# Decode attention kernel: closing barrier removed, output split into early and late DMAs (the last head by columns), identity matmul ahead of two V pieces

## The chip, the cores and the metric

The kernel runs on one core of one Trainium2 chip. The metric is the device time of one execution in microseconds (us). A profiled execution also has a span, from its first to its last record, which is 1 to 2 us shorter than the time. Engines are PE (matmul), PEld (its weight loads), DVE (vector), ACT (scalar), POOL (GpSimd) and SP, which here only issues DMAs; SPq is SP's queue of DMA issues.

## The reference

```python
B, Hq, Hkv, Sq, Sk, D = 1, 32, 8, 1, 65536, 128      # q, k, v in bfloat16
k = jnp.repeat(k, Hq // Hkv, axis=1); v = jnp.repeat(v, Hq // Hkv, axis=1)
scores = jnp.einsum("bhqd,bhkd->bhqk", q, k) * D ** -0.5
return jnp.einsum("bhqk,bhkd->bhqd", _softmax(scores), v)
```

K and V are 134 MB each and are read once. The output is 32 rows of 128 bfloat16, 8 KB.

## The kernel before

K and V of each of the 8 KV heads come in two blocks of 8 MB, so there are N = 16 blocks. A block is 256 "tiles" of 128 x 128. DVE transposes K, PE makes the scores, ACT takes them out of PSUM and exponentiates, PE multiplies by V. There are two K buffers but only one V buffer, so V is refilled behind PE. The last two V blocks (14 and 15) are loaded in halves: a half may be loaded as soon as PE has used that half of the block before. `pv_s` counts the halves that PE has used.

The parts that matter (cuts marked):

```python
KLAST = (64, 64, 64, 64)          # pieces of the last K block, in tiles
VLAST = (64, 32, 16, 8, 8)        # pieces of the second half of the last V block
NEND = 2                          # so many of them after the identity matmul
# ... SP, the load queue
        def load_v(i):
            if i < N - HALVED: ...            # whole block, once PE has used all of block i-1
            sp.wait_ge(pv_s, 2 * i - 1)       # first half of block i-1 used
            load(vbuf, vf, i, 0, TH, va_in)
            sp.wait_ge(pv_s, 2 * i)           # second half of block i-1 used
            ...
        load_k(0)
        for j in range(1, N + 1):
            if j < N:
                load_k(j)
            load_v(j - 1)
        sp.wait_ge(ox_s, 1)
        sp.dma_start(of.rearrange("h (a i) -> a h i", a=A), oX).then_inc(o_out, 16)
        sp.wait_ge(o_out, 16)
# ... PE, after its loop: adds the first block's rescaled sum to the accumulator
        pe.matmul(acc[:, 0:R], lhsT=ident, rhs=o2, start=False, stop=False)
        for n, a, b in list(pieces(VLAST, TH))[-NEND:]:
            pe.wait_ge(vlast_in[n], 16)
            values(range(a, b))
# ... DVE, last step of its loop over heads, then what follows the loop
                    dv.wait_ge(pv_s, h * (2 * C) + 2)             # ALL of block 14, for the last head
                    dv.tensor_copy(o1, acc[:, 0:R]).then_inc(co_s, 1)
        weigh(H - 1); divisor(H - 1)
        dv.wait_ge(pv_s, 2 * N)
        dv.tensor_tensor(oT[:, Hq - R:Hq], acc[:, 0:R], recip, ALU.mult).then_inc(fin_s, 1)
        dv.wait_ge(fin_s, H)
        dv.transpose(oX, oT).then_inc(ox_s, 1)
```

`oT` holds the output as columns, 128 partitions by 32 query rows. Blocks of 32 x 32 are transposed into `oX`, so that one DMA can write the output as 128 runs of 64 bytes. The engines' programs stand in a block with a barrier at its end.

Of the kernel before, what the change touches and what calls it, by code (L numbers as in the profile page):

```python
# [11 lines left out]
S4 = 32  # L12
T = 256
TG = 16
# [3 lines left out]
NK = 2  # L18
NKT = 2
FIRST = (64, 64, 128)  # L20
KLAST = (64, 64, 64, 64)
VLAST = (64, 32, 16, 8, 8)
NEND = 2
HALVED = 2


def bass_standalone__gqa_softmax__decode_kernel(nc, q, k, v, out):
    B, Hq, Sq, D = q.shape
    _, H, Sk, _ = k.shape
    R = Hq // H  # L30
    CK = P * T
# [4 lines left out]
    A = P // S4  # L36
    NB, NE = 2, 2
    W = T // U * R
    TH = T // 2
    QH = NB * NE * A * R  # L40
    scale = float(D) ** -0.5
    assert sum(VLAST) == TH and sum(VLAST[-NEND:]) == TG

    kf, vf = k[0], v[0]
    qf, of = q[0, :, 0, :], out[0, :, 0, :]

    es = ExitStack()
    S = es.enter_context
# [12 lines left out]
    oT, oX = oTX[:, 0:Hq], oTX[:, Hq:]  # L61
# [23 lines left out]
    def sem(name):  # L85
        return S(nc.semaphore(name))
# [3 lines left out]
    first_in = [sem(f"first_in{i}") for i in range(len(FIRST))]  # L90
    klast_in = [sem(f"klast_in{i}") for i in range(len(KLAST))]
    vlast_in = [sem(f"vlast_in{i}") for i in range(len(VLAST))]
    q_in, o_out = sem("q_in"), sem("o_out")
    tr_s, qk_s, mv_s, mx_s, hm_s = sem("tr_s"), sem("qk_s"), sem("mv_s"), sem("mx_s"), sem("hm_s")
    hma_s, nb_s, df_s, wg_s, ex_s, pv_s = sem("hma_s"), sem("nb_s"), sem("df_s"), sem("wg_s"), sem("ex_s"), sem("pv_s")
    ls_s, co_s, ow_s, rw_s, rh_s, rc_s, fin_s = (
        sem("ls_s"), sem("co_s"), sem("ow_s"), sem("rw_s"), sem("rh_s"), sem("rc_s"), sem("fin_s"))
    ox_s, tail_s = sem("ox_s"), sem("tail_s")
    init_s, pool_s, qt_s, qb_s, warm_s = sem("init_s"), sem("pool_s"), sem("qt_s"), sem("qb_s"), sem("warm_s")

    def src(t, i):
        h, c = divmod(i, C)
        return t[h, c * CK:(c + 1) * CK, :].rearrange("(p t) d -> p (t d)", p=P)

    def pieces(sizes, at=0):
        for n, size in enumerate(sizes):
            yield n, at, at + size
            at += size

    block = S(nc.Block())  # L110

    @block.sync
    def _(sp):
        def load(buf, t, i, a, b, s):
            sp.dma_start(buf[:, a * D:b * D], src(t, i)[:, a * D:b * D]).then_inc(s, 16)  # L115

        def load_k(i):
            if i >= NK:
                sp.wait_ge(tr_s, (i - NK + 1) * G)
            if i in (0, N - 1):  # L120
                for n, a, b in pieces(FIRST if i == 0 else KLAST):
                    load(kbuf[i % NK], kf, i, a, b, (first_in if i == 0 else klast_in)[n])
            else:
                load(kbuf[i % NK], kf, i, 0, T, k_in[i % NK])

        def load_v(i):
            if i < N - HALVED:
                if i >= 1:
                    sp.wait_ge(pv_s, 2 * i)
                load(vbuf, vf, i, 0, T, v_in)  # L130
                return
            sp.wait_ge(pv_s, 2 * i - 1)
            load(vbuf, vf, i, 0, TH, va_in)
            sp.wait_ge(pv_s, 2 * i)
            if i < N - 1:
                load(vbuf, vf, i, TH, T, vb_in)
            else:
                for n, a, b in pieces(VLAST, TH):
                    load(vbuf, vf, i, a, b, vlast_in[n])

        load_k(0)
        for j in range(1, N + 1):
            if j < N:
                load_k(j)
            load_v(j - 1)
        sp.wait_ge(ox_s, 1)
        sp.dma_start(of.rearrange("h (a i) -> a h i", a=A), oX).then_inc(o_out, 16)
        sp.wait_ge(o_out, 16)

    @block.gpsimd  # L150
    def _(g):
# [24 lines left out]
    @block.tensor  # L176
    def _(pe):
        def scores(g, qcols):


            kt = ktb[g % NKT][:, :].rearrange("p (b n e) -> p b e n", b=NB, e=NE)
            for n in range(TG // A):
                at = (g % GU * (TG // A) + n) * A * R
                for be in range(NB * NE):
                    ins = pe.matmul(  # L185
                        qkb[g // GU][:, at:at + A * R],
                        lhsT=kt[:, be // NE, be % NE, n * P:(n + 1) * P],
                        rhs=qblk[:, bass.ds(qcols[be], A * R)],
                        start=be == 0, stop=be == NB * NE - 1,
                    )  # L190
            ins.then_inc(qk_s, 1)

        def values(tiles):

            for t in tiles:
                ins = pe.matmul(  # L196
                    acc[:, 0:R], lhsT=vbuf[:, t * D:(t + 1) * D], rhs=pts[:, t * R:(t + 1) * R],
                    start=t == 0, stop=t == T - 1,
                )
                if t % TH == TH - 1:  # L200
                    ins.then_inc(pv_s, 1)


        turn, skip, skipl, late, last, kept, whole = (
            pe.alloc_register(name) for name in ("turn", "skip", "skipl", "late", "last", "kept", "whole"))
        pe.reg_mov(turn, 0)
        pe.wait_ge(qb_s, A * NB)
        with nc.Fori(
            0, N + 1, 1, engines=bass.OrderedEngineSet([pe.engine]), head_slot={pe.engine: 0},
        ) as it:  # L210
            pe.reg_alu(skip, it, 1, ALU.is_lt)
            pe.reg_alu(last, it, N, ALU.is_ge)
            pe.reg_alu(late, it, N - HALVED + 1, ALU.is_ge)
            pe.reg_add(skipl, skip, last)
            pe.reg_alu(kept, it, N - 1, ALU.min)
            pe.reg_alu(whole, it, N - HALVED, ALU.min)
            kept_ = pe.snap(kept, min_val=0, max_val=N - 1)
            whole_, late_, last_ = (pe.snap(r, min_val=0, max_val=N) for r in (whole, late, last))
            hq = kept_ // C * QH
            qcols = [hq + be * A * R for be in range(NB * NE)]  # L220
            with pe.If_lt(turn, N):
                for g in range(G):
                    if g % GU == 0:
                        pe.wait_ge(mv_s, it * U + (g // GU + 1))
                    pe.wait_ge(tr_s, it * G + (g + 1))
                    scores(g, qcols)
            with pe.If_eq(skip, 0):
                pe.wait_ge(co_s, it - 1)
                pe.wait_ge(ex_s, it * R)
                pe.wait_ge(v_in, whole_ * 16)  # L230
                pe.wait_ge(va_in, late_ * 16 + last_ * 16)
                values(range(TH))
                pe.wait_ge(vb_in, late_ * 16)
                for n, a, b in list(pieces(VLAST, TH))[:-NEND]:
                    pe.wait_ge(vlast_in[n], last_ * 16)
                    values(range(a, b))
            with pe.If_eq(skipl, 0):
                values(range(T - TG, T))
            pe.reg_add(turn, turn, 1)


        pe.wait_ge(tail_s, 2)
        pe.wait_ge(ow_s, H)
# [5 lines that stand above are left out]
    @block.vector  # L249
    def _(dv):  # L250
# [28 lines left out]
        def weigh(h):  # L279

            dv.wait_ge(wg_s, h + 1)
            dv.wait_ge(co_s, h * C + 1)
            dv.tensor_tensor(o2, o1, wgt, ALU.mult).then_inc(ow_s, 1)  # L283
            dv.wait_ge(ex_s, h * (R * C) + R * C)
            dv.tensor_tensor(rhead, rsum[0], wgt, ALU.mult).then_inc(rw_s, 1)  # L285
            dv.wait_ge(rw_s, h + 1)
            dv.tensor_tensor(rhead, rsum[1], rhead, ALU.add).then_inc(rh_s, 1)  # L287

        def divisor(h):
            dv.wait_ge(ls_s, h + 1)  # L290
            dv.reciprocal(recip, lsum).then_inc(rc_s, 1)  # L291
            dv.wait_ge(rc_s, h + 1)
# [4 lines left out]
        started, before, filled, last = (  # L297
            dv.alloc_register(name) for name in ("started", "before", "filled", "last"))


        with nc.Fori(0, H, 1, engines=bass.OrderedEngineSet([dv.engine]), head_slot={dv.engine: 0}) as h:  # L301
# [8 lines left out]
            for b in range(C):  # L310
                dv.wait_ge(k_in[b], (filled_ if b else h) * 16)
                moved = h * (C * U) + (U + b * U + 1)
                for g in range(G):
                    for n, at, _ in pieces(KLAST if b else FIRST):
                        if at == g * TG:
# [21 lines left out]
                else:  # L337
                    with dv.If_eq(started, 1):
# [5 lines left out]
                        dv.wait_ge(co_s, h * C)  # L344
                        dv.tensor_tensor(oT[:, bass.ds(before_ * R, R)], o2, recip, ALU.mult).then_inc(fin_s, 1)  # L345

        weigh(H - 1)
        divisor(H - 1)
        dv.wait_ge(pv_s, 2 * N)
        dv.tensor_tensor(oT[:, Hq - R:Hq], acc[:, 0:R], recip, ALU.mult).then_inc(fin_s, 1)  # L350
        dv.wait_ge(fin_s, H)
        dv.transpose(oX, oT).then_inc(ox_s, 1)

    @block.scalar
    def _(ac):
# [68 lines left out]
```

## Time and profile before

| | before |
|---|---|
| time, first three runs | 631.56 us median (630.2 to 631.56) |
| span | 628.3 us |
| moved | 268.60 MB, 427 GB/s over the span |
| busy PE, DVE, ACT | 43%, 54%, 44% |

The executions fall into two groups 1.3 us apart (630.2 and 631.5). Differences below 1 us are therefore hard to see.

The page's view in 40 equal slices has the busy share of the DMA engines in tenths, and the rate in GB/s:

```profile
DMA  9999999999999999999999999999999999999996
GB/s 368 438 445 427 439 430 438 430 438 430 438 426 442 426 442 421 446 421 446 421 446 421 446 421 446 421 446 421 446 421 446 421 446 421 446 396 429 437 427 277
```

The loads never pause until the last slice. No compute engine is busy throughout (DVE, the busiest, has 54%), so the load stream bounds the kernel, and only its start, a hole in it, or what follows its last byte can move the time.

The windows view shows the busy time of the engines in chosen stretches; the last two columns are the DMA share and rate. Around the moment when block 14 is used up:

```profile
604.00:606.00 2.00, 0.66 (x24) 0.66 (x25) 0.00 (x0) 0.00 (x0) 0.00 (x0) 1.00 0.99 426
606.00:608.00 2.00, 2.00 (x81) 2.00 (x79) 0.00 (x0) 0.00 (x0) 0.00 (x0) 1.00 1.10 475
608.00:610.00 2.00, 0.92 (x35) 0.83 (x32) 0.32 (x2) 1.04 (x3) 0.00 (x0) 1.00 0.87 377
610.00:612.00 2.00, 0.00 (x0) 0.00 (x0) 0.00 (x0) 2.00 (x6) 0.00 (x0) 1.00 1.07 459
```

PE works on the second half of block 14 while the first half of block 15 is already arriving.

The timeline shows start, length, engine, line and what the engine had waited for. Single rows of the last 30 us:

```profile
599.24 0.33 SPq L115 DMA_DIRECT2D vbuf<-in_v_dram  x1
...
605.34 3.58 PE L196 MATMUL acc<-pts,vbuf 128*128 128x4 bf16 x128 [6.14 <-DMA vbuf<-in_v_dram]
...
615.06 3.57 PE L196 MATMUL acc<-pts,vbuf 128*128 128x4 bf16 x128 [6.14 <-DMA vbuf<-in_v_dram]
...
622.45 1.01 PE L196 MATMUL acc<-pts,vbuf 128*128 128x4 bf16 x32 [0.55 <-DMA vbuf<-in_v_dram]
...
624.38 0.56 PE L244 MATMUL acc<-small,ktb 128*128 128x4 f32 x2
...
624.79 0.57 PE L196 MATMUL acc<-pts,vbuf 128*128 128x4 bf16 x16
625.47 0.16 DVE L350 TENSOR_TENSOR oTX<-acc,small 128x4 bf16<-128x4 f32 x1 [12.32 <-PE acc L196]
625.66 0.21 DVE L352 STREAM_TRANSPOSE oTX<-oTX 128x32 bf16<-128x32 bf16 x1
625.90 0.67 SPq L147 DMA_DIRECT2D out_dram<-oTX  x1
```

The first half of block 15 is issued at 599.24 us, six microseconds before the last half of block 14 lands at 605.3. After the last matmul (625.36) come a multiply, a transpose, the output DMA and the end at 628.3: 2.9 us. The waits of SP's queue (total us, times, longest us) give the landing of the output and the closing barrier:

```profile
SPq L395 <- DMA out_dram<-oTX: 1.3, 1, 1.3
...
SPq L395 <- PEq L395: 0.2, 1, 0.2
```

### The profile page before, as it was taken

Reading aid. Unit: us, or ns where it says so; the run is one execution under the profiler, and the core shown is the slowest. Engines: PE = TensorE matmul, PEld = TensorE weight load, DVE = VectorE, ACT = ScalarE, POOL = GpSimd, SP = SyncE. Lnnn points to the kernel's source line nnn. Section 1 sums busy time; section 2 is a strip of 40 time slices with the busy share of each in tenths; the row PEclk is TensorE's granted clock in tenths of the full one; section 3 lists DMA queues with packets and bytes.
Section 4 is the critical chain, followed back from the end, with each engine's and each line's share of the span. In section 5 each row is a group of like instructions: output and inputs, shape, how many; then the busy total and the mean of one; then the engine's idle time right before and its main releaser. Section 6 shows DMA issues by size and latency. Waiting matters only on the chain.

```text
span 628.3 us, 19296 instructions
## 1 busy us (share of the span) xinstructions
PE 270.1 (43%) x8194; PEld 244.0 (39%) x8194; DVE 341.0 (54%) x411; ACT 275.6 (44%) x1178; POOL 10.5 (2%) x32
## 2 busy tenths in 40 slices
PE   0325537144361534625345252552615536147535
PEld 0314536144361433614335252452514526146434
DVE  1868376290853908448094470935719266195810
ACT  0365535164351734607346172551625526164730
POOL 0000000000000000000000000000000000000000
DMA  9999999999999999999999999999999999999996
GB/s 368 438 445 427 439 430 438 430 438 430 438 426 442 426 442 421 446 421 446 421 446 421 446 421 446 421 446 421 446 421 446 421 446 421 446 396 429 437 427 277
DMA packets 6526, 268.60 MB, mean 427 GB/s; under 512 B 1012, under 2 KB 1012, under 8 KB 1396
## 3 DMA queue, kind: packets, MB, share of 16 engines
q1 hardware_dynamic: 6324, 268.45, 99.0%
q8 instruction: 5, 0.08, 0.1%
q10 hardware_dynamic: 192, 0.03, 0.0%
q14 instruction: 5, 0.04, 0.0%
HBM read 268.47 MB, written 0.01 MB: 427 GB/s over the span
## 4 chain that ended last, share of the span: by engine, by line
DMA 63%; DVE 16%; issue 10%; PE 9%; SPq 0%; DVEq 0%; ACTq 0%
DMA kbuf<-in_k_dram 55%; DVE ktb L267 14%; PE acc L196 9%; DMA vbuf<-in_v_dram 7%; DVE small L274 1%; DMA scs<-in_q_dram 1%; PE qkb L185 1%; SPq L115 0%; ACTq L357 0%; DVE qblk L262 0%; DVEq L320 0%; DVEq L318 0%; PE acc L244 0%; DVE scs L254 0%; DVEq L301 0%
## 5 line engine op out<-in xcount | busy, mean ns | idle before, releaser
L267 DVE STREAM_TRANSPOSE ktb<-kbuf 128x1024 int32<-128x1024 int32 x256 | 295.6, 1212 | 153.9 <-DMA kbuf<-in_k_dram 144.6
L367 ACT ACTIVATE scs<-qkb 32x64 f32<-32x64 f32 x1024 | 220.3, 215 | 278.3 <-PE qkb L185 267.1
L185 PE MATMUL qkb<-qblk,ktb 128*128 x4096 | 157.2, 176 | 339.4 <-DVE ktb L267 328.9
L185 PEld LDWEIGHTS qkb<-qblk,ktb 128*128 128x128 bf16 x4096 | 132.7, 105 | 363.7 <-issue 201.1
L196 PE MATMUL acc<-pts,vbuf 128*128 128x4 bf16 x4096 | 112.5, 166 | 15.7 <-DMA vbuf<-in_v_dram 15.1
L196 PEld LDWEIGHTS acc<-pts,vbuf 128*128 128x128 bf16 x4096 | 111.1, 104 | 17.5 <-DMA vbuf<-in_v_dram 14.1
L274 DVE TENSOR_REDUCE small<-scs 128x4 f32<-128x256 f32 x64 | 37.5, 586 | 61.4 <-ACT scs L367 61.4
L390 ACT ACTIVATE pts<-scs,small 128x256 bf16<-128x256 f32 x64 | 48.9, 853 | 32.5 <-PE acc L196 32.2
L162 POOL PARTITION_ALL_REDUCE small<-small x16 | 5.9, 372 | 587.9 <-DVE small L329 587.9
L390 ACT ACTIVATION_READ_ACCUMULATOR pts<-scs,small 128x1 f32 x64 | 13.6, 213 | 0.0
L378 ACT ACTIVATE small<-small 128x4 f32<-128x4 f32 x16 | 3.3, 205 | 22.5 <-POOL small L162 22.5
L336 DVE COPY small<-acc 128x4 f32<-128x4 f32 x8 | 1.3, 161 | 21.2 <-PE acc L196 21.2
L342 DVE TENSOR_TENSOR small<-acc,small 128x4 f32<-128x4 f32 x7 | 1.1, 162 | 13.8 <-PE acc L196 13.8
L350 DVE TENSOR_TENSOR oTX<-acc,small 128x4 bf16<-128x4 f32 x1 | 0.2, 162 | 12.3 <-PE acc L196 12.3
L254 DVE STREAM_TRANSPOSE scs<-scs 128x64 int32<-128x64 int32 x1 | 0.2, 245 | 9.8 <-DMA scs<-in_q_dram 9.8
L329 DVE TENSOR_REDUCE small<-small 128x4 f32<-128x16 f32 (+1 forms) x16 | 3.0, 185 | 1.3
L154 POOL PARTITION_ALL_REDUCE small<-small x8 | 3.4, 431 | 13.4 <-DVE small L287 13.4
L334 DVE TENSOR_TENSOR small<-small 128x4 f32<-128x4 f32 x8 | 1.3, 163 | 4.0 <-POOL small L162 4.0
L285 DVE TENSOR_TENSOR small<-small 128x4 f32<-128x4 f32 x8 | 1.3, 162 | 2.7 <-ACT pts L390 2.7
L360 ACT ACT_TABLE_LOAD x1 | 1.3, 1283 | 3.0 <-issue 3.0
L345 DVE TENSOR_TENSOR oTX<-small 128x4 f32 x7 | 1.1, 163 | 1.7 <-DVE small L291 1.7
L283 DVE TENSOR_TENSOR small<-small 128x4 f32<-128x4 f32 x8 | 1.4, 180 | 0.9
(18 smaller groups left out, 8.8 us busy)
## 6 DMA issues: line engine op xcount, KB each, us to landing
kbuf<-in_k_dram SPq DMA_DIRECT2D x6, 2048.0 KB, 37.5
vbuf<-in_v_dram SPq DMA_DIRECT2D x3, 4096.0 KB, 24.8
kbuf<-in_k_dram SPq DMA_DIRECT2D x1, 4096.0 KB, 22.8
vbuf<-in_v_dram SPq DMA_DIRECT2D x1, 2048.0 KB, 11.0
vbuf<-in_v_dram SPq DMA_DIRECT2D x1, 1024.0 KB, 13.1
vbuf<-in_v_dram SPq DMA_DIRECT2D x1, 512.0 KB, 13.9
vbuf<-in_v_dram SPq DMA_DIRECT2D x2, 256.0 KB, 14.1
kbuf<-in_k_dram SPq DMA_DIRECT2D x14, 49.8
```

Source lines behind the costliest of these rows:

```text
L154: g.partition_all_reduce(lsum, rhead, P, bass.bass_isa.ReduceOp.add).then_inc(ls_s, 1)
L162: g.partition_all_reduce(mtot if b else mfirst, hmax[:, b * R:(b + 1) * R], P, bass.bass_isa.ReduceOp.max,).then_inc(hma_s, 1)
L185: ins = pe.matmul(qkb[g // GU][:, at:at + A * R], lhsT=kt[:, be // NE, be % NE, n * P:(n + 1) * P], rhs=qblk[:, bass.ds(qcols[be], A * R)] ...
L196: ins = pe.matmul(acc[:, 0:R], lhsT=vbuf[:, t * D:(t + 1) * D], rhs=pts[:, t * R:(t + 1) * R], start=t == 0, stop=t == T - 1,)
L267: dv.transpose(to.rearrange("p (b t j) -> p b t j", b=NB, t=TG), fr.rearrange("p (t b i) -> p b t i", b=NB, t=TG),).then_inc(tr_s, 1)
L274: dv.tensor_reduce(hp[b][:, u * R:(u + 1) * R], scs[:, u * W:(u + 1) * W].rearrange("p (n g) -> p g n", g=R), AX.X, ALU.max,).then_inc(mx_ ...
L283: dv.tensor_tensor(o2, o1, wgt, ALU.mult).then_inc(ow_s, 1)
L285: dv.tensor_tensor(rhead, rsum[0], wgt, ALU.mult).then_inc(rw_s, 1)
L329: dv.tensor_reduce(hmax[:, b * R:(b + 1) * R], hp[b].rearrange("p (u g) -> p g u", g=R), AX.X, ALU.max,).then_inc(hm_s, 1)
L367: ins = ac.activation(to[a * S4:(a + 1) * S4, x, :, :], fr[x * S4:(x + 1) * S4, a, :, :], AF.Copy)
L378: ac.activation(negb[b], mtot if b else mfirst, AF.Copy, scale=-scale).then_inc(nb_s, 1)
L390: ac.activation(pv[:, g_, :], sv[:, g_, :], AF.Exp, bias=negb[b][:, g_:g_ + 1], scale=scale, accum_out=rsum[b][:, g_:g_ + 1],).then_inc(ex ...
```

## The change

Its intent is to shorten what follows the last byte. The diff is shortened. Seven of the eight heads are finished long before the end, so their rows go out early; the last head needs no transpose if it goes out by columns, straight from `oT`; the identity matmul moves ahead of the last two pieces, now of 16 and 8 tiles; the barrier goes.

```diff
-KLAST = (64, 64, 64, 64)
-VLAST = (64, 32, 16, 8, 8)
+KLAST = (128, 128)
+VLAST = (72, 32, 16, 8)
 NEND = 2
+class Straight: ...        # the engines' programs without a block
-    block = S(nc.Block())
+    block = Straight(nc)
         for j in range(1, N + 1):
             if j < N:
                 load_k(j)
+            else:
+                sp.wait_ge(ox_s, 1)
+                for a in range(A):
+                    rows = slice(a * S4, a * S4 + Hq - R)
+                    sp.dma_start(of[0:Hq - R, a * S4:(a + 1) * S4], oX[rows, :]).then_inc(o_out, 16)
             load_v(j - 1)
-        sp.wait_ge(ox_s, 1)
-        sp.dma_start(of.rearrange("h (a i) -> a h i", a=A), oX).then_inc(o_out, 16)
-        sp.wait_ge(o_out, 16)
+        sp.wait_ge(fin_s, H)
+        with nc.allow_non_contiguous_dma(reason="the last head goes out by columns"):
+            sp.dma_start(of[Hq - R:Hq, :].rearrange("h d -> d h"), oT[:, Hq - R:Hq]).then_inc(end_s, 16)
+        sp.wait_ge(o_out, 16 * A)
+        sp.wait_ge(end_s, 16)
# PE: the pieces after the identity matmul (TE tiles in all) may now be more than 16
-                values(range(T - TG, T))
+                values(range(T - TE, T))
# DVE, after its loop
+        dv.wait_ge(fin_s, H - 1)
+        dv.transpose(oX, oT).then_inc(ox_s, 1)
         weigh(H - 1)
         divisor(H - 1)
         dv.wait_ge(pv_s, 2 * N)
         dv.tensor_tensor(oT[:, Hq - R:Hq], acc[:, 0:R], recip, ALU.mult).then_inc(fin_s, 1)
-        dv.wait_ge(fin_s, H)
-        dv.transpose(oX, oT).then_inc(ox_s, 1)
```

More of the change, by code (lines that the diff above doesn't have):

```diff
@@ L20, with __init__ @@
 FIRST = (64, 64, 128)
-KLAST = (64, 64, 64, 64)
-VLAST = (64, 32, 16, 8, 8)
+KLAST = (128, 128)
+VLAST = (72, 32, 16, 8)
 NEND = 2
 HALVED = 2
+class Straight:
+    def __init__(self, nc):
+        self.sync, self.gpsimd, self.tensor, self.vector, self.scalar = (
+            lambda f, e=e: f(e) for e in (nc.sync, nc.gpsimd, nc.tensor, nc.vector, nc.scalar))
 def bass_standalone__gqa_softmax__decode_kernel(nc, q, k, v, out):
@@ L41, in bass_standalone__gqa_softmax__decode_kernel @@
     scale = float(D) ** -0.5
-    assert sum(VLAST) == TH and sum(VLAST[-NEND:]) == TG
+    TE = sum(VLAST[-NEND:])
+    assert sum(VLAST) == TH
     kf, vf = k[0], v[0]
@@ L92, in bass_standalone__gqa_softmax__decode_kernel @@
     vlast_in = [sem(f"vlast_in{i}") for i in range(len(VLAST))]
-    q_in, o_out = sem("q_in"), sem("o_out")
+    q_in, o_out, end_s = sem("q_in"), sem("o_out"), sem("end_s")
     tr_s, qk_s, mv_s, mx_s, hm_s = sem("tr_s"), sem("qk_s"), sem("mv_s"), sem("mx_s"), sem("hm_s")
```

## The prediction

> **What bounds the kernel now.** The DMA stream. The page gives 268.6 MB at 427 GB/s over a 628.3 us span, and the DMA row of the 40 slices reads 9 in all but the last. DVE is 54% busy, PE 43%, ACT 44%. So only three things move the time: when the stream starts, holes in it, and what follows its last byte.
>
> The timeline of the last 60 us (before): V block 14 lands in halves at 595.6 and 605.3 us, the first half of block 15 at 615.06, the last pieces by about 624.35. The stream has no hole, because the first half of block 15 is issued at 599.24, when PE has used the first half of block 14, six microseconds before the queue would run dry. After the last byte: identity matmul 0.56 us, 16 value matmuls to 625.37, DVE multiply 0.16, transpose 0.21, output DMA issued 625.90 (0.67), a wait of 1.3 for it, and the closing barrier; end 628.31, 3.96 us after the last byte.
>
> **What the change gains, all after the last byte.** Identity matmul ahead of two pieces (now 16 and 8): about 0.4 us. Transpose off the tail: 0.2 to 0.25. No closing barrier: the wait list shows some tenths of a microsecond; I take 0.3. Branches into the blocks at the start: 0 to 0.2.
>
> **What it adds there.** The last head goes out as 512 elements of 2 bytes, where before 128 rows of 64 bytes took about 0.3 us of packets. The Trainium skill ("DMA: Bandwidth & Descriptors", "Rules for kernel authors") says that a strided last dimension becomes one descriptor per element; no trace here shows it yet. Four times the packets at the same rate is 1.2 us, an estimate: plus 0.9, perhaps plus 2. The tail is a draw: 0 ± 1 us.
>
> **What it moves, and this decides.** The output DMAs of the first seven heads stand on SP's queue ahead of both halves of V block 15, behind a wait for the DVE transpose. That transpose comes after DVE's loop, whose last step copies the accumulator once PE has used ALL of block 14: 608.96 before. The first half of block 15, which needed only the first half of block 14, is now held too. Expected: PE done 608.93, copy 608.96, transpose about 609.2 to 609.4, four issues of about 0.45 each (four issues took 2.01 at the start), so block 15 is issued near 611.4 instead of 599.24. The queue is empty from 605.3. At the start, data began about 0.8 us after the issue, and the ramp lost some 0.6. Hole: 605.3 to about 612.8, 7.5 us, all on the critical path. The remaining 8.4 MB take 19 us as before, so the last byte comes near 632 instead of 624.35.
>
> The K pieces of 128 tiles delay the last block's scores by an estimated 1 to 2 us (halves land near 576 and 586, DVE started at 574.96); slack hides this, since PE must wait for 605.3 anyway.
>
> **Prediction:** +7.5 us hole, tail about 0: 638.8 us, 80% range 636.3 to 642.5; about 1.2% slower. Faster by over 2%: 0.01; within 2%: 0.94; slower by over 2%: 0.05.
>
> **What would show it.** The DMA row drops near the end; over 605 to 613 us the windows show a rate near zero; the SP waits list a V load waiting on DVE's transpose; the chain of waits passes from PE's block 14 through DVE and SP's output issues to V; PE's wait for the first half of block 15 grows from 6.2 to about 14 us; the tail after the last byte stays 3 to 5 us.
>
> **What would make it wrong.** Two-byte writes costing several microseconds (slower); slow issues of the 28-row outputs; a faster ramp or quicker end than I assume; a start gain from the missing branches.

## The result, and the profile after

| | before | after |
|---|---|---|
| time, median of fast runs | 630.88 us (4 runs) | 649.45 us (4 runs, 648.98 to 650.72) |
| ratio | | 1.0301, 95% interval 1.0283 to 1.0318 |
| span | 628.3 us | 648.4 us |

Ratios, here and below, are the mean time of one kernel's fast runs over that of the other's of the same rounds, so they are not quite the ratio of the medians quoted. Executions over 1.5% slower than the fastest of the same kernel are left out of the means.

The changed kernel is 18.6 us slower, and outside the predicted range of 636.3 to 642.5. The slices of the page show two losses:

```profile
DMA  9999999999999999999999999999999999999490
GB/s 383 448 418 434 425 425 441 420 441 445 416 441 437 441 420 433 449 412 445 441 416 441 437 441 420 433 449 412 445 441 416 441 437 441 410 425 441 193 418 3
```

One slice of 16 us at 193 GB/s is a hole in the stream. The last slice, again 16 us, moves nothing to speak of. The windows of the hole, and of the end, of the changed kernel:

```profile
604.00:606.00 2.00, 0.79 (x29) 0.79 (x30) 0.00 (x0) 0.00 (x0) 0.00 (x0) 1.00 0.00 0
606.00:608.00 2.00, 2.00 (x81) 2.00 (x79) 0.00 (x0) 0.00 (x0) 0.00 (x0) 1.00 0.00 0
608.00:610.00 2.00, 0.79 (x30) 0.70 (x27) 0.43 (x3) 1.18 (x3) 0.00 (x0) 1.00 0.00 0
610.00:612.00 2.00, 0.00 (x0) 0.00 (x0) 0.08 (x1) 1.88 (x6) 0.00 (x0) 1.00 0.34 86
...
634.50:635.00 0.50, 0.00 (x0) 0.00 (x0) 0.00 (x0) 0.00 (x0) 0.00 (x0) 1.00 0.51 2
635.00:636.00 1.00, 0.00 (x0) 0.00 (x0) 0.00 (x0) 0.00 (x0) 0.00 (x0) 1.00 0.00 0
636.00:648.40 12.40, 0.00 (x0) 0.00 (x0) 0.00 (x0) 0.00 (x0) 0.00 (x0) 1.00 0.00 0
```

From 604 to 610 us nothing is loaded; in finer windows, not shown, the packets stop by 603.5 us and flow again from about 611.8. At the end, the 2-byte packets are all done within the half microsecond from 634.5 to 635.0 (2 GB/s there is the 1 KB of the last head). For the remaining 13 us the profile shows no engine and no DMA engine busy. The timeline shows who held the loads, and the waits of SP's queue show what the end waits for:

```profile
608.82 0.16 DVE L352 COPY small<-acc 128x4 f32<-128x4 f32 x1 [6.85 <-PE acc L212]
609.01 0.21 DVE L365 STREAM_TRANSPOSE oTX<-oTX 128x32 bf16<-128x32 bf16 x1
...
609.25 1.65 SPq L158 DMA_DIRECT2D out_dram<-oTX  x4
...
610.94 2.39 SPq L124 DMA_DIRECT2D vbuf<-in_v_dram  x5
...
623.13 3.57 PE L212 MATMUL acc<-pts,vbuf 128*128 128x4 bf16 x128 [14.35 <-DMA vbuf<-in_v_dram]
...
632.54 0.83 PE L212 MATMUL acc<-pts,vbuf 128*128 128x4 bf16 x24
...
633.66 0.40 SPq L162 DMA_DIRECT2D out_dram<-oTX  x1
```

```profile
SPq L158 <- DVE oTX L365: 34.7, 1, 34.7
...
SPq L164 <- DMA out_dram<-oTX: 14.3, 1, 14.3
```

The first half of block 15 is issued at 610.94 instead of 599.24, and PE starts on it at 623.13 instead of 615.06: 8.1 us later. The output's landing is waited for 14.3 us instead of 1.3. In the span, PE's last matmul ends 8.0 us later (633.37 against 625.36), and the stretch after it grows from 2.9 to 15.0 us, by 12.1 us; together that is the 20.1 us by which the spans differ.

### The profile page after: what moved, and what is told of

Its sections match the earlier page's. It is cut to its first block, busy times and chain, and to the rows that moved or that the text cites. A ratio compares the mean times of both kernels' runs of the same rounds, so it can differ in the third digit from the quotient of the medians.

```text
span 648.4 us, 19286 instructions
## 1 busy us (share of the span) xinstructions
PE 269.9 (42%) x8194; PEld 244.0 (38%) x8194; DVE 341.0 (53%) x411; ACT 275.6 (43%) x1178; POOL 10.5 (2%) x32
## 2 busy tenths in 40 slices
DMA packets 6658, 268.60 MB, mean 414 GB/s; under 512 B 1528, under 2 KB 1528, under 8 KB 1784
## 4 chain that ended last, share of the span: by engine, by line
DMA 62%; DVE 16%; PE 10%; issue 9%; SPq 1%; DVEq 0%; ACTq 0%
DMA kbuf<-in_k_dram 53%; DVE ktb L283 14%; PE acc L212 8%; DMA vbuf<-in_v_dram 8%; PE qkb L201 2%; DVE small L290 1%; DMA scs<-in_q_dram 1%; SPq L124 0%; SPq L158 0%; ACTq L374 0%; DVE qblk L278 0%; DVEq L336 0%; DVEq L334 0%; PE acc L260 0%; DVE scs L270 0%
## 6 DMA issues: line engine op xcount, KB each, us to landing
kbuf<-in_k_dram SPq DMA_DIRECT2D x2, 2048.0 KB, 10.3
vbuf<-in_v_dram SPq DMA_DIRECT2D x1, 256.0 KB, 20.1
```

## The experiments

My theory after the result: two losses that add, the hole (SP's order of issue) and the landing of the 2-byte writes. The rivals: the slow end comes from the missing barrier or from the early output DMAs; the hole comes from the K pieces. The first two runs each undo one part of the change.

### e1_rows_end: the last head by 64-byte rows again

```diff
 # SP, in the changed kernel, in place of the write by columns
+        sp.wait_ge(ox_s, 2)
+        sp.dma_start(of.rearrange("h (a i) -> a h i", a=A), oX).then_inc(end_s, 16)
 # DVE, after the last multiply
+        dv.wait_ge(fin_s, H)
+        dv.wait_ge(o_out, 16 * A)
+        dv.transpose(oX, oT).then_inc(ox_s, 1)
```

> The changed kernel with the last head written by 64-byte rows after a second transpose (one output DMA of all heads, as the kernel before had it), the early output DMAs kept where they stand. Theory (two losses: 7 to 8 us hole in the load stream, 11 to 13 us landing of the 2-byte writes): the hole stays, the landing shrinks from 14.7 us to 2 to 3, time about 638.5 us. Rival 1 (the slow end comes from the missing barrier or from the early output DMAs still being in flight, not from the 2-byte writes): the wait for the last output stays above 10 us and the time stays near 649.

Measured: correct, 637.75 us (637.55 to 638.03) against 630.58 for the kernel before, ratio 1.0113 (1.0096 to 1.0129). The wait of SP's queue for the output:

```profile
SPq L163 <- DMA out_dram<-oTX: 1.4, 1, 1.4
```

The barrier is still missing and the early outputs are still there, and the landing is back to 1.4 us. So the rival for the end falls, and the slow landing belongs to the write by columns. The hole stays: PE starts on the first half of block 15 at 623.33, and the kernel is 7.2 us slower than before.

```profile
623.33 3.58 PE L211 MATMUL acc<-pts,vbuf 128*128 128x4 bf16 x128 [14.32 <-DMA vbuf<-in_v_dram]
```

### e2_heads_after_v: the early outputs behind the V loads

```diff
             if j < N:
                 load_k(j)
-            else:
-                (wait for ox_s, four output DMAs)
             load_v(j - 1)
+        (wait for ox_s, four output DMAs)
```

> The changed kernel with the four early output DMAs issued after the loads of the last V block; the last head still by 2-byte columns. Theory: the hole from 604 to 612 us is gone, first half of block 15 lands near 615 again, and about 12 us of slow landing stay: time 641 to 642 us. Rival (the hole comes from something else, such as the K pieces of 128 tiles delaying the scores): the hole stays and the time stays near 649.

Measured: correct, 640.89 us (640.35 to 641.91) against 630.58, ratio 1.0165 (1.0148 to 1.0182). The windows of this run where the hole was, PE's start on block 15, and the wait for its output:

```profile
606.00:608.00 2.00, 2.00 (x82) 2.00 (x78) 0.00 (x0) 0.00 (x0) 0.00 (x0) 1.00 0.87 377
608.00:610.00 2.00, 0.75 (x29) 0.66 (x25) 0.43 (x3) 1.21 (x3) 0.00 (x0) 1.00 0.95 410
```

```profile
614.90 3.57 PE L211 MATMUL acc<-pts,vbuf 128*128 128x4 bf16 x128 [6.15 <-DMA vbuf<-in_v_dram]
```

```profile
SPq L163 <- DMA out_dram<-oTX: 13.4, 1, 13.4
```

The hole is gone with the order of issue alone, although the last K block still comes in two pieces. PE starts on block 15 at 614.90. The slow landing stays. The two runs are slower than the kernel before by 7.2 and 10.3 us. Each of them also keeps the gain of the missing barrier (1 us, below), so in their sum, 17.5 us, that gain is taken off twice; with one of the two given back it is 18.5 us, against the whole change's 18.6.

### e3, e4, e9, e10, e12: what makes the 2-byte writes slow

These five edit only the last output DMA of the changed kernel. Their outputs are wrong, which doesn't matter for the times. Only the wait for the landing is read.

```diff
 # the changed kernel: 512 elements, by columns, into 4 rows of 256 bytes
  of[Hq - R:Hq, :].rearrange("h d -> d h"),  oT[:, Hq - R:Hq]
 # e3: one row only, 128 elements
+ of[Hq - R:Hq - R + 1, :].rearrange("h d -> d h"),  oT[:, Hq - R:Hq - R + 1]
 # e4: 512 elements spread over the whole output, every eighth element
+ of.rearrange("h (b x) -> (h b) x", x=S4)[:, 0:S4:S4 // R],  oT[:, Hq - R:Hq]
 # e9: the same 4 rows as the changed kernel, but 32 neighbours from each of 16 partitions
+ of[Hq - R:Hq, :].rearrange("h (b x) -> (h b) x", x=S4),  oTX[0:4 * R, 0:2 * Hq:2]
 # e10: by columns, every second element, 256 elements
+ of[Hq - R:Hq, 0:P:2].rearrange("h d -> d h"),  oT[0:P // 2, Hq - R:Hq]
 # e12: 512 elements, the first 64 bytes of each of 16 rows
+ of[0:4 * R, 0:S4],  oTX[0:4 * R, 0:2 * Hq:2]
```

> Wrong on purpose: only one of the last four query rows is written by 2-byte columns (128 elements, and each 64-byte stretch still takes 32 of them). If all 2-byte writes go through one after the other (about 26 ns each), the landing falls from 14.7 us to about 4.5. If instead the writes to the same 64 bytes wait for each other while different stretches go in parallel, it stays near 14.7 us. If it is a fixed cost of any such DMA, it also stays.

> Wrong on purpose: the same 512 elements of 2 bytes, but spread over the whole output, four to each 64-byte stretch and each stretch from one partition. If writes to one stretch (or one small neighbourhood) wait for each other, the landing falls from 14.7 us to 2 to 5. If 2-byte writes are slow by their number alone, it stays near 14.7 us.

> Wrong on purpose: 512 elements of 2 bytes into the same four rows of the output, 32 to each 64-byte stretch as in the changed kernel, but written one stretch after the other's order by stretch, not by column, so that neighbours of a stretch follow each other. If what counts is how many 2-byte writes fall on one stretch, the landing stays at 13 to 15 us. If what counts is that writers of different partitions take turns on a stretch, it falls to 2 to 5 us.

> Wrong on purpose: columns as in the changed kernel, but every second element only: 256 writes of 2 bytes, 16 to each 64-byte stretch. If the cost goes with the number of writes on a stretch, about 0.4 us each, the landing falls from 14.7 to about 8 us. If it is a fixed cost once stretches are shared, it stays near 14.

> Wrong on purpose: 512 elements of 2 bytes, filling the first 64 bytes of each of 16 output rows: 32 writes to each 64-byte stretch as in the changed kernel, but 32 and not 128 to each 256-byte row. If the unit on which such writes wait for each other is 64 bytes or smaller, the landing stays at 13 to 15 us; if it is 128 bytes, about 7 to 8; if 256 bytes or more, about 4 to 5.

The waits for the output landing, one kernel to a fence, in the order e3, e4, e9, e10, e12:

```profile
SPq L164 <- DMA out_dram<-oTX: 15.6, 1, 15.6
```

```profile
SPq L164 <- DMA out_dram<-oTX: 2.9, 1, 2.9
```

```profile
SPq L164 <- DMA out_dram<-oTX: 13.1, 1, 13.1
```

```profile
SPq L164 <- DMA out_dram<-oTX: 6.7, 1, 6.7
```

```profile
SPq L164 <- DMA out_dram<-oTX: 5.1, 1, 5.1
```

(The expectations speak of the time from issue to landing; this wait starts when the issue has ended and is 0.3 to 0.7 us shorter.) Set side by side:

| run | 2-byte writes | per written 64 bytes | per written 256-byte row | wait, us |
|---|---|---|---|---|
| changed kernel | 512 | 32 | 128 | 14.3 |
| e3_one_row | 128 | 32 | 128 | 15.6 |
| e9_one_engine | 512 | 32 | 128 | 13.1 |
| e10_every_second | 256 | 16 | 64 | 6.7 |
| e12_first_quarters | 512 | 32 | 32 | 5.1 |
| e4_scatter | 512 | 4 | 16 | 2.9 |

The number of writes does not set the wait: a quarter of the writes took as long (e3), and the same number took a fifth as long (e4). How crowded the writes lie does. When each 64-byte stretch is written from one partition alone (e9), little changes, so it is not partitions taking turns on a stretch. The first four experiments left open over which length the writes crowd; I had believed in 64 bytes, and e12 contradicts that, because it has 32 writes on each 64 bytes and waits only 5.1 us. A length beyond one row is contradicted by e3, where one full row alone waits as long as four. Of the columns here, the one of the 256-byte row orders all six runs.

A stretch of 128 bytes is not excluded: it would hold 64 writes in the first three rows of the table, 32 in e10 and e12, and 8 in e4, which orders the runs too. In e12 the time from issue to landing, 5.5 us, lies nearer to what was expected for 256 bytes (4 to 5) than for 128 (7 to 8), but no run settles it.

From e4 to the changed kernel the wait grows by (14.3 - 2.9) / (128 - 16) = 0.10 us for each further write on a row. That is a line through two runs with one look each, not a mechanism: it gives 4.5 us for e12 and 7.8 for e10, where 5.1 and 6.7 were measured, and the three runs with 128 writes on a row differ by 2.5 us among themselves. Whether the row itself counts, or how many DMA engines write to one row at once, these patterns don't tell apart.

### e5_no_barrier: only the barrier and the block removed from the kernel before

```diff
-    block = S(nc.Block())
+    block = Straight(nc)
```

> The kernel before without its closing barrier and block branches, nothing else. Prediction's term: 0.3 us less at the end, 0 to 0.2 less at the start, so 630.1 to 630.5 against about 630.6; ratio 0.999 to 1.0. Rival (the missing barrier itself costs time): over 631.5.

Measured: correct, 629.34 us (629.3 to 630.68) against 630.3; ratio 0.9988 (0.9974 to 1.0003). It is a gain of 1.0 us by the medians, with an interval that just holds 1. The span falls from 628.3 to 628.0 us, as predicted, and the wait for PE's queue at the end is gone from the list. The rest lies outside the span: the profiled executions took 630.11 us for a span of 628.3, and here 629.31 for 628.0, so 1.8 us outside the span became 1.3. All fast runs of the two kernels show the same two figures, within 0.05 us. I had not counted that part.

### e6_identity and e8_both_gains: the moved identity matmul

```diff
-VLAST = (64, 32, 16, 8, 8)
+VLAST = (72, 32, 16, 8)
-                values(range(T - TG, T))
+                values(range(T - TE, T))     # e8: the same, and no barrier
```

> The kernel before with the V pieces 72, 32, 16, 8 and the identity matmul ahead of the last two, nothing else. Prediction's term: about 0.4 us less, all between the last byte and the last matmul; ratio about 0.9994. Rival (the piece of 72 tiles landing later eats it): no gain.

> Candidate: the kernel before with only the missing barrier and the moved identity matmul; output by 64-byte rows in one DMA as before, loads in the order of before. Theory: the two gains add, 0.6 to 1 us, about 629.8; faster than both kernels but inside 2%. If the gains do not add: about 630.2 or no change.

Measured: e6 630.27 us against 630.3, ratio 0.9998 (0.9984 to 1.0013); e8 629.62 us, ratio 0.9989 (0.9975 to 1.0003), the same as e5. The move brings nothing. PE's last rows of e6 in the timeline:

```profile
623.17 1.01 PE L197 MATMUL acc<-pts,vbuf 128*128 128x4 bf16 x32 [0.34 <-DMA vbuf<-in_v_dram]
...
624.21 0.56 PE L245 MATMUL acc<-small,ktb 128*128 128x4 f32 x2
...
624.62 0.79 PE L197 MATMUL acc<-pts,vbuf 128*128 128x4 bf16 x24
```

In the kernel before PE still waits for a piece after the 32-tile one. Here it waits last for the 32-tile piece, which now ends at tile 104 of the half instead of 96 and lands at 623.17 instead of 622.45. From there PE has 2.2 us of work without a pause, the identity matmul among it, and ends at 625.41, as before at 625.36. The matmul was moved within PE's backlog, not out of it.

### e7_k_halves: only the K pieces

```diff
-KLAST = (64, 64, 64, 64)
+KLAST = (128, 128)
```

> The kernel before with its last K block loaded in two pieces of 128 tiles, nothing else. Theory: the scores of the last block end 1 to 2 us later, hidden by the slack of the V loads; time unchanged within 0.3 us. Rival (this change shifts the end too): 1 to 2 us longer.

Measured: correct, 630.65 us (630.04 to 631.36), two executions in each of the two groups, ratio 1.0002 (0.9986 to 1.0017). The expectation holds within the noise. In e2, which has the same pieces, PE reached block 14 1.1 us later than in the kernel before (596.71 against 595.63) and still had to wait for its second half.

### e11_identity_first: a candidate

The e5 kernel with the identity matmul ahead of all five pieces, where PE is idle anyway.

```diff
-NEND = 2
+NEND = 5
-                values(range(T - TG, T))
+                values(range(T - TE, T))
```

> Candidate: the kernel before without its closing barrier, its V pieces kept at 64, 32, 16, 8, 8, and the identity matmul ahead of all five of them, in the idle time of PE after the first half of the block. Theory (identity matmul was worth nothing ahead of two pieces because PE was already behind the loads from the third-last piece on): the last matmul ends about 0.4 to 0.5 us sooner after the last byte, time about 628.9, ratio about 0.998. Rival (the end is set by the last piece's landing alone): as without barrier only, 629.3.

Measured: correct, 629.44 us (629.3 to 629.85) against 630.31, ratio 0.9979 (0.9965 to 0.9993). It is faster than both kernels, by about 0.2%. Its median is not better than that of e5 (629.34), so moving the matmul this far adds nothing that these runs show; what is left is the gain of the missing barrier and block, and the rival expectation held. In its profile (the slowest of its five executions) the identity matmul does run in the idle stretch, and PE then waits for the last piece:

```profile
619.36 0.56 PE L253 MATMUL acc<-small,ktb 128*128 128x4 f32 x2 [0.24 <-issue]
...
625.47 0.37 PE L205 MATMUL acc<-pts,vbuf 128*128 128x4 bf16 x8 [0.26 <-DMA vbuf<-in_v_dram]
```

Once PE has no backlog, the landing of the last piece sets the end.

## Why the prediction was wrong

- **"Hole: 605.3 to about 612.8, 7.5 us, all on the critical path."** The mechanism is right: PE's start on block 15 moved by 8.1 us, and e2 shows that the order of issue is its cause. The predicted issue at 611.4 was 610.94; PE's wait of "about 14 us" was 14.35. But I took the landing of block 14 (605.3) for the end of the stream. Its packets stop by 603.5 us and flow again from about 611.8; both ends were put too late, and these errors nearly cancel, so the close size is partly luck.
- **"plus 0.9, perhaps plus 2"** for the write of 2-byte elements. This is the step that failed. The term measured plus 13 us (14.3 against 1.3), and e1 shows that it belongs to this write: without it, 637.75 us were measured, against the 638.8 that I had predicted for the whole change. I had costed the write by its packets, and the packets are indeed cheap: all done within 0.5 us. The cost is the time between the last packet and the landing, which no packet count shows. I took the kernel before's 1.3 us wait for a constant. What the hardware does in that time is not shown. The prediction did list "Two-byte writes costing several microseconds" among what would make it wrong, but its sum had no such term.
- **"the tail after the last byte stays 3 to 5 us"** Wrong for the same reason; after PE's last matmul alone, which follows the last byte, it was 15.0 us.
- **"Identity matmul ahead of two pieces (now 16 and 8): about 0.4 us."** Mis-sized: e6 measures nothing, because the pieces changed with it and PE's backlog stayed.
- **"Transpose off the tail: 0.2 to 0.25."** Right: from the last multiply to the output's issue it was 0.43 us before (625.47 to 625.90) and 0.19 after (633.47 to 633.66).
- **No closing barrier 0.3, branches 0 to 0.2.** About right in the span (0.3 us together); another 0.5 us came outside the span. By the medians it is 1.0 us.
- **The K pieces delay the scores by 1 to 2 us, and slack hides this.** Right (1.1 us, hidden).

The text cited from the Trainium skill, "DMA: Bandwidth & Descriptors", section "Rules for kernel authors", that a strided last dimension becomes one descriptor per element. This trace agrees: the page's count of packets under 512 B is 1528 in the changed kernel, and 1144, 384 fewer, in e3, which writes 384 elements fewer. The same page has two passages that bear on the failed step and that I did not use. Its "Specifications" say that below 512 B a DMA does a read-modify-write. No run here shows whether that is the cause, and runs of 64 bytes, which are below 512 B too, waited only 1.3 us. Its section "Anatomy of one DMA — SWDGE (gpsimd) path" says of the semaphore update that it can't fire until "the *last byte is confirmed landed* in the target memory". That section describes DMAs issued from another engine, but the trace, issued from SP, fits it: packets done by 635.0 us, semaphore at 648.4. The page gives the whole fixed cost as about 2 us; for runs of 64 bytes 0.67 us of issue and 1.3 us of wait agree, for crowded 2-byte writes 14.7 us from issue to landing do not.

## What to carry to other kernels

A DMA that waits in a queue holds everything issued behind it (here the first half of block 15, by 11.7 us): before putting an early output ahead of loads, find the latest semaphore it waits for, and compare it with what the next load needs. Don't cost a small write by its packets alone; read the wait for its landing, and keep the writes of one output row in few long runs, even if that takes one more transpose (0.21 us here). And when a piece of work is moved forward in a queue, check that the engine idles where it lands; within a backlog the move is worth nothing.

## What the Trainium skill lacked or had wrong

- "DMA: Bandwidth & Descriptors" names read-modify-write below 512 B and a fixed cost of about 2 us, but not that many 2-byte writes crowded on one stretch of the output delay the landing: 14.3 us for 512 elements filling four 256-byte rows, 15.6 for 128 elements filling one, 2.9 for 512 elements spread over the whole 8 KB, 1.3 for 128 runs of 64 bytes over the same 8 KB. About 0.10 us for each further write on a 256-byte row roughly fits the runs; a stretch of 128 bytes is not excluded.
- The same page's rule on strided last dimensions speaks of the number of descriptors. Here their number was not what cost: 512 packets took under 0.5 us, and the wait after them was 13 us.
- No page has the price of the closing barrier and the block it belongs to: 0.3 us in the span and 0.5 us outside it (1.0 us by the medians, 95% interval of the ratio 0.9974 to 1.0003).
